# A hand-fixed order written anew, with all table sums left to TensorE, in a gated mix of a state-space convolution and linear attention

## The chip, the cores and the metric

The kernel runs on one core of one Trainium2 chip. The metric is the device time of one execution in microseconds; the median of several runs is what counts. The engines of the core are TensorE (PE in the profile, with its weight loads as PEld), VectorE (DVE), ScalarE (ACT), GpSimd (POOL) and SyncE (SP), which here only issues DMA transfers. ACT issues some DMAs too.

## What is computed

A sequence `u` of 2048 steps by 512 channels goes through two branches, and a sigmoid gate per step mixes them. Cut to what matters:

```python
# convolution branch: a kernel K of length 2048 per channel, from 128 modes
P = exp(dt * A[d, n] * l)                       # complex, n = 128, l = 0..2047
K = einsum("dn,dnl,dn->dl", C, P, dt * B).real
y = irfft(rfft(u, 2L) * rfft(K, 2L))[:L] + u * Dskip
# attention branch: 32 heads of 16, features of 32
q, k, v = x @ wqkv
phi(t) = concat(softmax(t @ w_phi), softmax(-t @ w_phi))
kv = einsum("sf,sd->fd", phi(k), v); z = phi(k).sum(s)
b = (phi(q) @ kv) / (phi(q) @ z + 1e-6) @ wo
return g * y + (1 - g) * b,  g = sigmoid((u * gate_w).sum(-1))
```

## The kernel before

The program first turns the parameters into tables, transforms `u` (PE products with small matrices of sines and cosines in place of an FFT), and makes the key side of the attention in 8 **key pairs** of two 128-step tiles. Then four **query blocks** of 512 steps run, and beside them the convolution: the 512 channels are 16 **units** of 32 channels, and four units make a **quarter** of 128 channels, which is transformed and multiplied as one (the last quarter is cut in 64, 32 and 32 channels).

One unit goes like this. PE makes arguments, ACT turns them into sines and cosines (`cs`, line 1023 and behind) and into exponentials (`E`, line 1045 for the arguments). DVE makes two products `A` of the tables C and D (line 1101, twice 1.2 us: nodes A1, A2), then adds the two halves of `A` (line 1112: node A3) or leaves that away, and makes two products `R` of `E` and `cs` (lines 1119 and 1123). PE multiplies `A` by `R` into the PSUM tile `kps` (line 183, in `kgen_chunk`): 64 small matmuls where A3 has added the halves, 128 where PE sums four terms itself. The flag `FOURS`, one digit per unit, says which. Two units share one `kps`, which is evicted into `KD`. From there on: `psA` (PE) into `XA`, `psB` (PE) into `XK`, DVE's product `t` of `XK` with the transform of `u` read back from DRAM (`XUX`, line 1233), `psz` (PE) into `Zr`, written to DRAM and read back as `ZT` (line 1287), then `psy` (PE, line 1343) and DVE's product with the gate into `xT` (lines 1365 and 1368), from which rows go out (line 1382). The last query block does its output in `bps` (line 946) and sends its rows from line 995.

In a key pair PE makes `pk`, ACT the exponentials `Ek`, and these are summed over the features of a head, into `Zk`: by two DVE reductions (line 736), or by 8 matmuls with the identity into `zk` (line 730) and one narrower reduction (line 739). The flag `ZPS`, one digit per pair, says which.

Every step is a node of the class `Plan`. No scheduler runs: `ORDER` lists all nodes in base 64, two characters each, and each engine executes its instructions in that order. `SIDES` picks the engine of each node that has a choice: evictions of PSUM on ACT or DVE (lines 149 and 151 in `copy`), output DMAs on SP or ACT, a few preparatory operations on DVE or POOL. `RINGS` picks which of two rings of PSUM buffers a tile is taken from. Buffers are counted in the line

```python
P = Plan(nc, {"XAu": 1, "UDp": 1, "xst": 2, "wT": 1, "Ek": 2, "Zk": 2, "vr": 2, "vb": 2, "acc": 1, "r8": 3, "ax": 1, "nrm": 1, "E": 2, "cs": 4, "A": 1, "R": 2,
              "KD": 1, "XA0": 1, "XK": 2, "Zr": 2, "XUX": 3, "ln": 8}, {"ps": 2, "p0": 2, "bk": 3, "acc": 1, "pf": 2})
```

so there is one buffer for `A`, two for `E`, `R`, `XK` and `Zr`, four for `cs`. The query blocks' tile `ax` shares its one buffer with `ZT`.

Of the kernel before, what the change touches and what calls it, by code (L numbers as in the profile page):

```python
# [70 lines left out]
class Plan:  # L71

    DIGITS = "0123456789abcdefghijklmnopqrstuvwxyzABCDEFGHIJKLMNOPQRSTUVWXYZ-_"
    ORDER = ("040B0H0K0d0y0C0D0L0s0I070J0M0P0g000S110j0N08010z0T0m0Q0e2R0a0p0q0r0_0W2T100U0O0V14120Y2U2x0A2S050k130Z2y2V2X2Z0R190v0t0u"
             "0b0c0w2_0l0E0X2W1516172L1a061b2Y022-30311y33340n030f0-"
             "0h1e1f0i1w2J18321c0F0o2B2K2M1n1z1H1g1A1o2D2C1d1p1I091x1E1J351Q1R2F1B0x1C2E0G2H1q36372G2I2P382N2Q391F3b2O3c4C1S3a4J4L4K4M"
             "3d3e4Q4R3f4U1Y3g4N1r4O1h4V3h1L4Y4-"
             "4P3i4Z4_3j4W4S53542z57504T3k4X1Z515b5d58521s1D593l5c3n5i5e55565j3m5a1G3o5q5f5g5s5r5t3p3r3q1T5m5n5u3s5v5h5o5k5w5x5B1P4D4E"
             "3w2v5l5p4F5y5F5C3y1U5H3x5G5I5J5z5A1V5D5E3t3z5U3D5K5V5M5N3A3R3E2w3F5W5L1O5_3G5O5Q5X5Y5Z3B3C1W605R5S1N3K3M1K3S1M5-"
             "5P3L634G642A615T653N673T6869626a666m6n6o3U6p3V3W3X3Y6b6c6q6d6r6s1t3Z3H3-1X3_3O1i1j41401_4221431-"  # L80
             "1k1l204445466e272923222b282d4748243P491m2a4a2c2e4b4g2f4c2g4d252h2o4e4h4i4n1u4j3u3v2j4p2i2l2k2m2q2p6i262s4q4o1v4k2n4u2r2t"
             "6f4v4w6j4r3I2u4x4y4z6g4l8l3J4A8p8m6t6u6k6v8q3Q4f4s6x6h8k8o6l8n8r8s6y6z6w6A6C4m4t4B8C6G8t6I6K8w8x8y8u6B6H6J4H8D8v6L6M6N7d"
             "8z8A8E4I8B7e7f8I7g8F6F9e8Q8G8H9b6O6P8R7h7j7i6Q6R8J9f7M7N8S6S6T6U6Vaeaf7O8W8X8K7k9g8L8T8U8Z8-"
             "938M8N7l6D8_7m8V7n6W6X6Y8O8P8Y7P94an7o7pao7q6_70717r90917Qa47S9295ag7R6Z7s6-"
             "72aha8a9966Ea7akaca5ai73aa75979998ajap7677a69aalatamab74ad7TaBaC7t797u7v7U78au7y7z7V7w7x9caq9naras7AavaH7W9d9h9o9paw7X9v"
             "aY9waK7Y7ZaDaL9q9raZ7a9x9y9zaIc57B7-aM9kc69D9EaQaEbX9L7Cb_aF7D9M7_9Ac07EaRaG9iaxaz80ay9B818285bYaA7Ga-"
             "7IaJ86879j9Fc19s7Jb-"
             "9l9m9Na_7bc7aNaOaPc3cbb2b37HbZc283aS9C7FaT849G9H9I9t89aUaWaV8baX7cccc8c99O9u9P9Q9R888cb87Kb9b0c4caceb19J8abacfcgbg8dck9K"
             "8ecl8f8gbbbh8hbcbibob4cP9Sbpbqcd9T8ichci7L8jcBcCcjcsdYcYctcucycDczdZd-cQcR9Ucmd_cHcvcw9W9Xcnbj9VbwbkblbxcocIbre0eLcp9Ze1"
             "e2b5b6eMbse3eUeVcxb7bye4cqbtbu9Ybdbe9-"  # L90
             "9_cAcrcSbme5cZdOdScEbfcFcGcTcUe6a0a1bve7dTdRdWeNa2e8cJcKe9bzbAedeecLeRcNcOa3eSeaebeOcMc_ePbBd0ecd1d7cVd8d9cWeCdfcXeWdPdU"
             "d2daefege-e_eQd3dbdQdgeTdVd4dndodXdhdcg1g2dieDeEdjeXbKfAbCbnbDbEbFeYfBeZf0f1bGc-dpbLddg7dqbHd5f2drbMf3f4f5bNfGbIbJbOezdk"
             "eAfDdsfEeBeIf6f7feffdldtbPdebQdBfCfHehdueifFejdmf8fgeJd6ekdvfIfJdyf9fafhfbg4fifKg5g6dwfjdzfkfcdxdCdEfLdAdFfMg3g8dGg9dHfN"
             "fleFelfdfmfpdDdLgagbgcgddIeGemeKfqeHfOfPfQfRgeenepfneofreqeresgfggghgifSfTfUfofsbRgjbSgkdJftetglfVfYfZgmgngobUbVgqfufWdM"
             "dNbWgpf-fvfxfygreufwevewexbTeydKfzfXf_g0gvgwgsgtgugx")
    SIDES = ("011111010010101011001110110010011001010100001011100000000000011000011001111101000100000100000000000000000000000010000000"
             "00100001000000000000000101010000000000000100001101001")
    RINGS = ("001010111111010010100000000000000000000000100000000000000000001101100000000101101011100100100001101010111100111001010100"
             "01111")
# [560 lines left out]
def attention_keys(P, nc, g, psum, r):  # L660
# [40 lines left out]
    for s2 in range(8):  # L701
# [20 lines left out]

        def ps4(K=K, box=box, on=P.ZPS[s2] == "1"):
            if not on:
                return
            box.ps = bank("zk")
            for u in range(2):
                e = K.E[:, u].rearrange("p g (h a b) -> p (g h) a b", a=4, b=4)
                for k in range(4):
                    nc.tensor.matmul(box.ps[:, 256 * u:256 * u + 256], lhsT=g.ident[:], rhs=e[:, :, k, :], start=(k == 0), stop=(k == 3), skip_group_check=True)  # L730

        def rd(K=K, box=box, on=P.ZPS[s2] == "1"):
            K.Z = g.kwk.tile([128, 2, 2, 32], F32, name="Zk")
            if not on:
                for u in range(2):
                    nc.vector.tensor_reduce(out=K.Z[:, u].rearrange("p g h -> p (g h)"), in_=K.E[:, u].rearrange("p g (h f) -> p (g h) f", f=16),
                                            axis=mybir.AxisListType.X, op=ALU.add)
                return
            nc.vector.tensor_reduce(out=K.Z[:].rearrange("p u g h -> p (u g h)"), in_=box.ps[:].rearrange("p (z b) -> p z b", b=4), axis=mybir.AxisListType.X, op=ALU.add)
            box.ps = None  # L740
# [294 lines left out]
def plan_exp(P, nc, g, psum, U, T, psq, deps):  # L1035

    act = g.act
    h, cc = U // 2, U % 2
    box = Bag()

    def pe():
        T.E = g.epool.tile([128, 2, 32, 32], BF16, name="E", bufs=g.P.k["E"])
        box.ps = psum([128, 2, 16, 32], "args")
        for e in range(2):
            nc.tensor.matmul(box.ps[:, e], lhsT=g.statE[64 * e:64 * e + 64, h, :], rhs=g.selE[64 * e:64 * e + 64, 16 * cc:16 * cc + 16, :],  # L1045
                             start=True, stop=True, tile_position=(64 * e, 0))
# [12 lines left out]

def plan_conv(P, nc, g, psum, r):  # L1060
# [567 lines left out]
```

## Time and profile before

| | before |
|---|---|
| median of 3 runs | 268.72 us (266.31, 268.72, 269.62) |
| span of the profiled execution, first to last instruction | 263.7 us |
| DVE busy | 233.9 us (89%) |
| ACT busy | 221.3 us (84%) |
| PE busy | 198.5 us (75%) |
| PE weight loads | 133.8 us |
| POOL busy | 8.3 us |
| moved by DMA | 35.93 MB, 136 GB/s on the mean |

The profile is that of one execution; its span is the time from its first to its last instruction, and the device time of the runs lies some us above it. Busy times are sums over one engine's instructions, so engines that run beside each other both count. In the prediction a row of the groups reads: line, engine, operation, output and input with their sizes, count, then busy us and mean ns of one, then the idle time just before them and what ended it. A row of waits reads: who waits, for whom, us in total, times, the longest. A row with two times in front is one run of instructions: when it starts (us from the start of the span) and how long it takes. SPq and ACTq are the DMA-issuing part of these engines.

### The profile page before, as it was taken

How to read it: one execution, taken by the hardware profiler on the slowest of the kernel's cores; microseconds unless marked ns; L12 is line 12 of the kernel's file. 1: busy time of each engine (PE TensorE's matmuls, PEld its weight loads, DVE VectorE, ACT ScalarE, POOL GpSimd, SP SyncE). 2: the span in 40 equal slices, each digit the busy share in tenths (PEclk: the TensorE clock that was granted, in tenths of full speed). 3: DMA queues.
4: the chain of work that ended last, by engine and by line, in shares of the span. 5: the costliest groups of instructions: out<-in, count | busy, mean ns of one | idle time of the engine just before them, and what ended most of it. 6: DMA issues, size and time to landing. Idle time of an engine off the chain costs nothing.

```text
span 263.7 us, 10050 instructions
## 1 busy us (share of the span) xinstructions
PE 198.5 (75%) x4491; PEld 133.8 (51%) x4512; DVE 233.9 (89%) x315; ACT 221.3 (84%) x305; POOL 8.3 (3%) x21
## 2 busy tenths in 40 slices
PE   0755999999845688988565867889996678979770
PEld 0654656646634423446354245665674456764550
DVE  6799989888799989999999999999999999986630
ACT  6989999998899989998999899999998996744200
POOL 4700000000000000000000000000000000000000
PEclk9999999999995659997999579999999999998975
DMA  6899000454500885203343366239753599989576
GB/s 196 144 204 233 6 4 2 121 146 138 151 10 2 239 239 165 83 13 87 88 162 82 122 209 210 73 116 199 150 193 120 189 239 242 179 206 141 133 112 102
DMA packets 67547, 35.93 MB, mean 136 GB/s; under 512 B 46000, under 2 KB 62000, under 8 KB 67504
## 3 DMA queue, kind: packets, MB, share of 16 engines
q1 hardware_dynamic: 65648, 34.76, 55.0%
q10 hardware_dynamic: 1856, 0.52, 1.1%
q8 instruction: 35, 0.57, 1.0%
q14 instruction: 8, 0.07, 0.1%
HBM read 22.17 MB, written 13.11 MB: 134 GB/s over the span
## 4 chain that ended last, share of the span: by engine, by line
PE 32%; DVE 26%; ACT 13%; DMA 12%; issue 7%; SPq 7%; DVEq 0%; ACTq 0%
PE pk L709 5%; DMA ax<-apd 5%; PE vp L757 5%; DVE A L1101 3%; SPq L1494 3%; DMA ZT<-Zd 3%; DMA apd<-apm 3%; ACT cs L68 3%; DVE R L1123 2%; DVE R L1119 2%; PE psz L1265 2%; PE psA L591 2%; PE bps L946 2%; PE psB L616 2%; PE kvp L774 2%
## 5 line engine op out<-in xcount | busy, mean ns | idle before, releaser
L1101 DVE TENSOR_TENSOR A<-Ctab,Dtab 128x2048 bf16<-128x2048 bf16 x32 | 37.9, 1220 | 0.0
L68 ACT ACTIVATE cs<-args 128x1024 bf16<-128x1024 f32 x32 | 30.8, 1042 | 1.5 <-PE args L1023 1.5
L1265 PE MATMUL psz<-t,TI 128*128 128x512 bf16 x51 | 16.5, 414 | 6.2 <-DVE t L1233 4.6
L1123 DVE TENSOR_TENSOR R<-E,cs 128x2048 bf16<-128x2048 bf16 x16 | 19.5, 1219 | 0.1
L1119 DVE TENSOR_TENSOR R<-E,cs 128x2048 bf16<-128x2048 bf16 x16 | 19.5, 1219 | 0.0
L68 ACT ACTIVATE Ek<-pk 128x512 bf16<-128x512 f32 x32 | 16.7, 600 | 1.9 <-PE pk L709 1.6
L183 PE MATMUL kps<-R,A 128*32 128x64 bf16 x1536 | 17.2, 203 | 1.5 <-DVE A L1112 0.4
L183 PEld LDWEIGHTS <-A 128*32 128x32 bf16 x1536 | 15.3, 117 | 5.6 <-issue 2.0
L149 ACT CAST Zr<-psz 128x1024 bf16<-128x1024 f32 x15 | 15.5, 1032 | 3.2 <-PE psz L1265 1.5
L149 ACT CAST XA<-psA 128x1024 bf16<-128x1024 f32 (+1 forms) x15 | 14.7, 1017 | 3.4 <-PE psA L190 3.4
L757 PE MATMUL vp<-WW,xT 128*128 128x512 bf16 x59 | 16.9, 419 | 0.5 <-issue 0.3
L616 PE MATMUL psB<-XAu,TB 64*128 64x128 bf16 x256 | 11.8, 250 | 6.6 <-ACT xst L149 3.5
L1233 DVE TENSOR_TENSOR t<-XUX,XK 128x2048 bf16<-128x2048 bf16 x14 | 16.7, 1219 | 0.0
L68 ACT ACTIVATE E<-args 128x1024 bf16<-128x1024 f32 x16 | 16.4, 1036 | 0.3 <-PE args L1045 0.2
L68 ACT ACTIVATE Eq<-pq 128x512 bf16<-128x512 f32 (+1 forms) x28 | 16.5, 694 | 0.1
L149 ACT CAST XK<-psB 128x1024 bf16<-128x1024 f32 (+1 forms) x14 | 13.7, 993 | 2.8 <-PE psB L196 1.5
L843 PE MATMUL pq<-xT,Wqp 128*128 128x512 bf16 x64 | 15.4, 379 | 0.8 <-ACT xT L149 0.6
L709 PE MATMUL pk<-WW,xT 128*128 128x512 bf16 x58 | 15.0, 380 | 0.4 <-issue 0.2
L190 PE MATMUL psA<-W,KD 128*64 128x128 bf16 x256 | 10.7, 233 | 5.5 <-ACT KD L149 2.7
L616 PEld LDWEIGHTS <-TB 64*128 64x128 bf16 x256 | 9.7, 111 | 9.9 <-issue 9.8
L196 PE MATMUL psB<-XA,TB 128*128 128x128 bf16 (+2 forms) x192 | 10.6, 206 | 3.6 <-DVE XA L151 1.6
L190 PEld LDWEIGHTS <-KD 128*64 128x64 bf16 x256 | 8.5, 117 | 9.1 <-issue 5.2
(210 smaller groups left out, 502.0 us busy)
## 6 DMA issues: line engine op xcount, KB each, us to landing
XUX<-XUd SPq DMA_DIRECT2D x32, 256.0 KB
XUd<-xst SPq DMA_DIRECT2D x8, 512.0 KB
ax<-apd SPq DMA_DIRECT2D x16, 256.0 KB
Zd<-Zr SPq DMA_DIRECT2D x15, 256.0 KB
ZT<-Zd SPq DMA_DIRECT2D x6, 512.0 KB
UD<-in_A_u_dram SPq DMA_DIRECT2D x16, 128.0 KB
XUd<-xst SPq DMA_DIRECT2D x8, 256.0 KB
wqk<-in_B_wqkv_dram SPq DMA_DIRECT2D x1, 1024.0 KB
```

Of the source, the lines that this page charges most:

```text
L68: return self.nc.scalar.activation(**kw)
L149: self.nc.scalar.copy(out=o, in_=i)
L183: nc.tensor.matmul(kps[32 * dj:32 * dj + 32, g4, e, :], lhsT=A[:, d // 4, 32 * ka:32 * ka + 32, d % 4], rhs=R[:, kr, d, :], start=(i == 0) ...
L190: nc.tensor.matmul(ps[64 * ri:64 * ri + 64], lhsT=lhsT, rhs=fc.W1[:, ri].rearrange("p r d -> p (r d)"), start=True, stop=True, tile_positi ...
L616: nc.tensor.matmul(box.ps[:, c2, sl, :], lhsT=fc.TB[rows, b0:b0 + 2].rearrange("p a b -> p (a b)"), rhs=X.t[rows, k, r0 + sl].rearrange("p ...
L709: nc.tensor.matmul(box.ps[:], lhsT=xT[:, st, kt, :], rhs=g.WW[:, kt, :], start=(kt == 0), stop=(kt == 3))
L757: nc.tensor.matmul(box.ps[:], lhsT=xT[:, st, kt, :], rhs=g.WW[:, 4 + kt, :], start=(kt == 0), stop=(kt == 3))
L1101: nc.vector.tensor_tensor(out=c.A[:, :, 64 * k:64 * k + 64, :].rearrange("p q (x b) l -> p x b q l", b=8), in0=cf.unsqueeze(2).to_broadcas ...
L1119: nc.vector.tensor_tensor(out=c.R[:, :, :, 32:64], in0=t.E[:, 1].unsqueeze(1).to_broadcast([128, 2, 32, 32]), in1=t.cs[:], op=ALU.mult)
L1123: nc.vector.tensor_tensor(out=c.R[:, :, :, 0:32], in0=t.E[:, 0].unsqueeze(1).to_broadcast([128, 2, 32, 32]), in1=t.cs[:, ::-1, :, ::-1], o ...
L1233: nc.vector.tensor_tensor(out=box.t, in0=Ls[r0 // ns].X[:], in1=box.XK[:].unsqueeze(1).to_broadcast([128, 2, 1024]), op=ALU.mult)
L1265: nc.tensor.matmul(box.ps[:, hb, :], lhsT=fc.TI[:, k].rearrange("p t h a -> p (t h a)"), rhs=box.t[:, k, 512 * hb:512 * hb + 512], start=( ...
```

## The change

`FOURS` becomes all ones, `ZPS` loses a one, and `ORDER`, `SIDES` and `RINGS` are new throughout. No other line changes; the tables take four lines less, so the lines behind them have numbers smaller by 4 in the changed kernel. The diff's core:

```diff
-    ORDER = ("040B0H0K0d0y0C0D0L0s0I070J0M0P0g000S110j0N08010z0T0m0Q0e2R0a0p0q0r0_0W2T100U0O0V14120Y2U2x0A2S050k130Z2y2V2X2Z0R190v0t0u"
...
+    ORDER = ("0H0I0s0t0u0J2L0K00190M0S0U0L0_0N110P1210130T0W0Q2x0O0B0C0D0V140g0h0i0Y0X2M0102032R2T150Z0y0z0A2J0405060R16171a2U2y0d0e0f"
...
     WARM = ("000000000000000000000000000000000000000000000000000000000000000000000000000000000000000000000000000000000000000000000000"
             "000000000000000000000")
-    FOURS = ("0111100101011000")
-    ZPS = ("01000111")
+    FOURS = ("1111111111111111")
+    ZPS = ("00000111")
```

Counted over the whole program, DVE has eight sums A3 fewer (line 1112), two reductions of line 736 more and one of line 739 fewer; PE has 512 `kps` matmuls more and 8 `zk` matmuls fewer; SP has the four DMAs of line 995 fewer and ACT has them; POOL has one operation more (`selE`, from DVE).

Three places show how the order moves. The first is VectorE near its end, the rows before the last product of the third quarter's output and the last unit; `R`, `A`, `E` and `t` are the products named above, `xT<-psy` is an output step. Before:

```order
L1365 TENSOR_TENSOR xT<-psy,gT 128x4x128
L1053 TENSOR_TENSOR E<-E,Gtab 128x1024
L1123 TENSOR_TENSOR R<-E,cs 128x64x32
L1112 TENSOR_TENSOR A<-A 128x8x256
L1233 TENSOR_TENSOR t<-XUX,XK 128x2048 x2
L1101 TENSOR_TENSOR A<-Ctab_75,Dtab 128x64x8x4 x2
L1112 TENSOR_TENSOR A<-A 128x8x256
L1053 TENSOR_TENSOR E<-E,Gtab 128x1024
L1123 TENSOR_TENSOR R<-E,cs 128x64x32
L1365 TENSOR_TENSOR xT<-psy,gT 128x4x128
L151 CAST XK<-psB 128x1024
L1368 TENSOR_TENSOR xT<-psy,gT 128x8x128
```

and with the change:

```order
L1049 TENSOR_TENSOR E<-E,Gtab 128x1024
L1097 TENSOR_TENSOR A<-Ctab_75,Dtab 128x64x8x4
L1361 TENSOR_TENSOR xT<-psy,gT 128x4x128
L1049 TENSOR_TENSOR E<-E,Gtab 128x1024
L1115 TENSOR_TENSOR R<-E,cs 128x64x32
L1119 TENSOR_TENSOR R<-E,cs 128x64x32
L1115 TENSOR_TENSOR R<-E,cs 128x64x32
L1229 TENSOR_TENSOR t<-XUX,XK 128x2048 x2
L1119 TENSOR_TENSOR R<-E,cs 128x64x32
L1097 TENSOR_TENSOR A<-Ctab_75,Dtab 128x64x8x4 x2
L1364 TENSOR_TENSOR xT<-psy,gT 128x8x128
L1361 TENSOR_TENSOR xT<-psy,gT 128x4x128
```

The two sums (line 1112) are gone, the `R` products of two units now stand together, and the pair of `A` products stands last of the table work instead of ahead of `E` and `R`.

The second is ScalarE round the last two exponentials (`E<-args`); `Zr`, `KD`, `XA` and `XK` are evictions on the path from `kps` to the output. Before:

```order
L68 ACTIVATE cs<-args 128x1024 x2
L149 CAST XK<-psB 128x1024
L65 ACT_TABLE_LOAD
L68 ACTIVATE E<-args 128x1024
L149 CAST Zr<-psz 128x2x8x64
L68 ACTIVATE E<-args 128x1024
L149 CAST KD<-kps 128x1024
L149 CAST Zr<-psz 128x2x8x64
L149 CAST XA<-psA 128x32x32 x2
L149 CAST XK<-psB 128x1024 x2
```

and with the change:

```order
L145 CAST oT_4861<-ops 128x1024
L145 CAST XK<-psB 128x1024
L68 ACTIVATE cs<-args 128x1024 x2
L65 ACT_TABLE_LOAD
L145 CAST Zr<-psz 128x2x8x64 x2
L68 ACTIVATE E<-args 128x1024
L145 CAST KD<-kps 128x1024
L68 ACTIVATE E<-args 128x1024
L145 CAST XA<-psA 128x32x32 x2
L145 CAST Ctab_74<-psy 128x4x128
L145 CAST XK<-psB 128x1024 x2
```

Both `Zr` evictions now stand ahead of the two exponentials, and `KD` between them.

The third is SyncE at its end; `Zd<-Zr` writes the third quarter's transform to DRAM, `ZT<-Zd` reads it back, `out_dram` are output rows. Before:

```order
L1278 DMA Zd_64_123<-Zr 128x1024
L1382 DMA out_dram<-xT 32x12x256 x2
L995 DMA out_dram<-xT 32x4x384 x2
L1287 DMA ZT<-Zd_64_123 64x32x32 x2
L1382 DMA out_dram<-xT 512x1x64 x4
L995 DMA out_dram<-xT 32x4x384 x2
L1382 DMA out_dram<-xT 512x1x64 x2
```

and with the change:

```order
L1378 DMA out_dram<-xT 32x12x128 x2
L1274 DMA Zd_64_123<-Zr 128x1024
L1378 DMA out_dram<-xT 32x12x128 x2
L1378 DMA out_dram<-xT 32x12x256 x2
L1283 DMA ZT<-Zd_64_123 64x32x32 x2
L1378 DMA out_dram<-xT 512x1x64 x6
```

The four transfers of line 995 are no longer on SyncE; they stand on ScalarE.

More of the change, by code (lines that the diff above doesn't have):

```diff
@@ L73 @@
     DIGITS = "0123456789abcdefghijklmnopqrstuvwxyzABCDEFGHIJKLMNOPQRSTUVWXYZ-_"
-    ORDER = ("040B0H0K0d0y0C0D0L0s0I070J0M0P0g000S110j0N08010z0T0m0Q0e2R0a0p0q0r0_0W2T100U0O0V14120Y2U2x0A2S050k130Z2y2V2X2Z0R190v0t0u"
[L75 to L99, printed above, removed]
+    ORDER = ("0H0I0s0t0u0J2L0K00190M0S0U0L0_0N110P1210130T0W0Q2x0O0B0C0D0V140g0h0i0Y0X2M0102032R2T150Z0y0z0A2J0405060R16171a2U2y0d0e0f"
+             "0j0k0l0a0b0c2S1y2V2X0708090m0n0o2K0-2Z0p0q0r1w2-1b1c1n2W0v0w0x1x1e1f2_1o1d1z1p1A2Y303118351g331q1r1s321H2B341B1E2C2H1I1C"
+             "1J362I2D371S1F2F2G1L2E2P1M2N382Q393b2O3a1D0E0F0G4C4J4L1Y1P3d3c4K3e3f4Y4M4N4O3g4Z4-3h4_1t1u1v1G4P4Q4U4R4S533j4V4W571T4T54"
+             "504X3i3k5b585c3l5d515259555e5i5j1Z5m5f5n3n3o5g565a5q5r3m5s5h4D5o5t5x3p5k5u5B1K5y4E1Q3r5l4F3q5v5p5F3R3s3t3u3v5w5C5D5H5z3w"
+             "3y5G5I3z1U5M5A5E5J5U3x3A3B3C5W5V5N5K5L2v2w3D3F3G5Q3S5O5X5_1h1i1j3K3T5R5S5Y3E635P603H3I3J5Z5-5T641R3M671N61621k1l1m696566"
+             "6m3L3U1V3N3V681W6o6a3W6n6p1O3X6b3Z3Y3O3P3Q3-6c6q4G3_6d6r6s4041424344451X1-201_272147464849222329284b6e242a4a2b2d4c2z254g"
+             "4i2f2c2e2o2A4d4e4f4j262g4h2h4k4l4m2i2q4n4o2j2p2k2l4p4q4r4s4t6t2s2m2r2t2n2u6f6u6v4u4w6x4x8n6g6i6j4v8r8l6h8p6y8k8o4y4z4A4B"
+             "6k6l6w6z6A8m8q6B6F4H4I7d8s8w6G8t8x8y8u6H8z8v6I6J9h9i9j8A8C8D8E6K8Q6L8I6M6N8B7f8F8J8R6O7e7g8G8S8Z9e9f9g6P8H7M7h7i8K7j6Q8W"
+             "8-6R6S8L6T7N6U6V6W8T8_8X8M8N7O7kae8O8Paf938U7l7m7Q7P9b9c9d8V6X6Y6Z8Y947n90anao7oa47p7R6_7071917qa8a99295ag7r7s7tap96a56-"
+             "ah72aaa7ac73ai6C6D6E75aka6at7u7v7waj7778749798ab79999aadalaB7SauamaC7x7Taq7y7z7A9n9o767UaD7Var9v9wasavaw9paK7WaL9q9xaH7a"
+             "9r9yaE9k9l9m9D7X7YaIaF7C9zaQaG7Z9s9t9u7E7F9E9L9Mc5c6axayazaAaMbXaJ7Ba_b0b1aRaN7Gb_7bc0aOaP7D7cbZc29Fcb9NaS7-7_8081828385"
+             "8687aT7I7J9G9HaUc8aVaWaXb-c38489c78bb87HbYb988bgaYaZa-9I9J9Kc18c7Kbhc98d8e9Obac4cc8f9Pcecacd9A9B9Ccfb2b3b4bick8aboch8g8h"
+             "bp7Lcgb5b6b7csci8iclcj8jctcybwdYd-cucm9Q9R9ScScTcU9T9U9VbxbqcvdZ9W9X9Ybbbjd_bce0cBbdbebfcne1czcCcwe29ZbkeUcHcoe3eVe4brcp"
+             "cDcPcQcRe5cxcIcqbyblbmbne6e7e8cAbscEcreLbtbubveMdOdS9-a0a1cFcGdTcYcZc-cJcK9_bzbAa2eWe9eaebeRcLcNcOcMc_eNa3d0d7dQd8dPeOd1"
+             "edeeefdfdUd2d9bBbCbDd3ecehcVcWcXegdgdneIeJeKdVd4d5d6dadbePeQbEbFbGeSeTdhe-eXeie_dRdodpdWdXdcdddedidjbHbIbJbKeYeZbLdqdrf0"
+             "g1bMg2fDdkdldmfAbNbOf1fBg3dsdtdufEeCeDeEf2bPf4f5f3bQfCejfGfFfHf6f7feezeAeBdvdwdxdBfffIg7f8fgfJf9fhfafig8g4g5g6dydzdAdCfK"
+             "fbfcfddEfLekdFfMfjfkfleFeGeHdDdGfNfObRbSbTg9dHgaelfmfnfofPgbgcfQfpfqfremgdgeepenfRdLdMdNfSfTfUdIdJdKgfeqerbUbVbWfsggghgi"
+             "gjgkgleogmgngoesfVfWfXfYfZf-ftfufvfwgqeteuevgpfxfyfzewexeygrf_g0gsgtgugvgwgx")
@@ L100 @@
+    SIDES = ("111101011110110010001000101000100001011100001101110000000000101010010001010100000011000100000001000000001000000000000000"
+             "01000001000000000000001000101100000000000100011000010")
+    RINGS = ("110000111110010000100000000000000000000000100000000000000010101111000000001100100101010110111011001100101011001111001011"
+             "11100")
     WARM = ("000000000000000000000000000000000000000000000000000000000000000000000000000000000000000000000000000000000000000000000000"
```

## The prediction

> **What bounds the kernel now.** The page comes first, for the engines' shares:
>
> ```profile
> span 263.7 us, 10050 instructions
> PE 198.5 (75%) x4491; PEld 133.8 (51%) x4512; DVE 233.9 (89%) x315; ACT 221.3 (84%) x305; POOL 8.3 (3%) x21
> ```
>
> VectorE (DVE) has the most work, ScalarE (ACT) only 12.6 us less. An average over stages says little, so the second view is the table of windows, cut where the first and the last table exponential (E, line 1045's `args`, evicted by ACT) start, and where the last `kps` ends:
>
> ```profile
> core 0: us, PE busy (x) PEld busy (x) DVE busy (x) ACT busy (x) POOL busy (x), PEclk, DMA share, GB/s
> 28.00:72.00 44.00, 42.91 (x752) 26.56 (x760) 38.60 (x53) 39.72 (x77) 0.00 (x0) 1.00 0.30 84
> ...
> 0.00:104.50 104.50, 78.46 (x1218) 51.44 (x1230) 93.47 (x162) 95.42 (x141) 8.33 (x21) 0.92 0.52 126
> 104.50:217.30 112.80, 87.38 (x2278) 58.00 (x2287) 110.88 (x120) 108.01 (x141) 0.00 (x0) 0.94 0.50 136
> 217.30:238.00 20.70, 18.05 (x547) 14.61 (x543) 19.37 (x19) 13.16 (x16) 0.00 (x0) 0.96 0.99 202
> 238.00:263.70 25.70, 14.66 (x472) 9.78 (x468) 10.21 (x16) 4.75 (x9) 0.00 (x0) 0.77 0.77 125
> ```
>
> The reader is to see four regimes. From 28 to 72 us (keys) PE is the full engine: 42.91 of 44. From 104.5 to 217.3 (table and convolution units) DVE is 98% busy, but ACT is 96% busy beside it: both are full at once. From 217.3 to 238.0 ACT has slack, DVE (19.37) and PE (18.05 of 20.7) have little. Behind 238 nobody is full: that is a chain of latencies. So a change that takes work from DVE alone is worth in the third row only what ACT allows, and in the fourth what PE allows. Third view, who waits for whom, ACT's rows between 104 and 217.3 us:
>
> ```profile
> ACT Zr L149 <- PE psz L1265: 1.5, 4, 0.6
> ACT XK L149 <- PE psB L196: 0.8, 1, 0.8
> ACT apm L68 <- DVE zs L886: 0.8, 2, 0.4
> ACT zs L68 <- PE zs L867: 0.7, 1, 0.7
> ACT XA L149 <- PE psA L190: 0.4, 2, 0.3
> ACT E L68 <- PE args L1045: 0.2, 1, 0.2
> ...
> PE psz L1265 <- DVE t L1233: 4.6, 5, 1.8
> PE psB L196 <- DVE XA L151: 1.6, 1, 1.6
> ```
>
> ACT idles 4.4 us there, and the last two rows (PE's, 104 to 238) say why PE was late for it: `psz` had waited for DVE's `t`, `psB` for DVE's XA eviction. So Zr 1.5, XK 0.8 and apm 0.8, 3.1 us together, come from a late DVE.
>
> **The change, part by part.** Rows by form:
>
> ```profile
> L1112 DVE TENSOR_TENSOR A<-A 128x2048 bf16<-128x2048 bf16 x8 | 9.8, 1221 | 0.1
> ...
> L1101 DVE TENSOR_TENSOR A<-Ctab,Dtab 128x2048 bf16<-128x2048 bf16 x32 | 37.9, 1220 | 0.0
> ...
> L736 DVE TENSOR_REDUCE Zk<-Ek 128x64 f32<-128x1024 bf16 x8 | 9.3, 1210 | 0.0
> ...
> L739 DVE TENSOR_REDUCE Zk<-zk 128x128 f32<-128x512 f32 x4 | 2.8, 692 | 1.4 <-PE zk L730 1.3
> ...
> L458 DVE TENSOR_TENSOR selE<-m,b 128x1024 bf16<-128x1024 bf16 x1 | 1.2, 1217 | 0.0
> ...
> L151 DVE CAST XAu<-psA 128x1024 bf16<-128x1024 f32 x8 | 9.5, 1218 | 1.5 <-PE psA L591 1.4
> ...
> L151 DVE CAST vb<-vp 128x512 bf16<-128x512 f32 x9 | 6.1, 687 | 1.9 <-PE vp L757 1.9
> ...
> L183 PE MATMUL kps<-R,A 128*32 128x64 bf16 x1536 | 17.2, 203 | 1.5 <-DVE A L1112 0.4 <-ACT XA L149 0.3 <-DVE A L1101 0.3
> ...
> L730 PE MATMUL zk<-Ek,ident 128*128 128x256 bf16 x32 | 4.2, 277 | 0.0
> ...
> L149 ACT CAST KD<-kps 128x1024 bf16<-128x1024 f32 x7 | 7.2, 1033 | 0.0
> ...
> L149 ACT CAST vb<-vp 128x512 bf16<-128x512 f32 x7 | 4.2, 596 | 1.2 <-PE vp L757 0.8 <-DVE vr L766 0.4
> ```
>
> DVE loses the eight sums on line 1112 (9.8 us) and selE (1.2, to POOL, which is busy 3%). The key pair that no longer goes over PE gives it two reductions of 1.21 for one of 0.69: +1.7. Of the evictions it gives up two wide ones (1.22 each) and seven narrow (0.69), and takes two wide, two narrow and three other copies, which I put at 0.75 each, near the narrow row: 6.1 for 7.3, -1.2. Sum **-10.5 us** of DVE work, -9.8 of it inside the units.
>
> ACT gets nothing from that. Counted by name in front of the last E, it has four wide evictions more (KD, XK, WW, a 1024-wide oT) and four fewer (two UDp, xT, XA), and three narrow more against one fewer: 2 x 0.6 = **+1.2 us** up to the last E; up to the first E the same count gives one wide more, three fewer, two narrow more: -0.8. The cover for ACT's unchanged load is nothing; it simply stays.
>
> PE gains 512 `kps` matmuls and loses 8 `zk`. By the row 17.2 / 1536 = 11.2 ns each, +5.7 and -1.05. The loss lies in the full key stage and agrees with ACT's -0.8 at the first E; I count it once. The gain lies beside ACT and DVE in a stage where PE is busy 87.38 of 112.8 us. What it costs if that cover is gone is a rival below.
>
> The Trainium skill, page "TensorE: Matmul & The Clock Gate", section "Wait — 56ns, not 53.3ns?", speaks against this change: matmuls never start closer than about 25 ns however small. An estimate by that page is 512 x 25 = 12.8 us instead of 5.7, 1.9 us more for each full unit, and with two units behind the last E a total of about 266 us. The trace disagrees: 128 `kps` in 1.26 us (row below) are 9.8 ns each, since four column strips run side by side; I keep the row.
>
> Now the path. The rows that carry it:
>
> ```profile
> 217.32 1.04 ACT L68 ACTIVATE E<-args 128x1024 bf16<-128x1024 f32 x1
> ...
> 115.88 1.26 PE L183 MATMUL kps<-R,A 128*32 128x64 bf16 x128
> ...
> 228.58 0.73 PE L183 MATMUL kps<-R,A 128*32 128x64 bf16 x64
> ...
> 241.73 1.04 PE L1265 MATMUL psz<-t,TI 128*128 128x512 bf16 x4
> ...
> 231.80 0.63 PE L1343 MATMUL psy<-ZT,TJ 64*32 64x128 bf16 x32
> ...
> 226.74 1.91 PE L932 MATMUL ops<-Eq,KVbd 128*128 128x256 bf16 x16
> ...
> 235.62 0.51 PE L1343 MATMUL psy<-ZT,TJ 64*32 64x128 bf16 x22 [1.43 <-issue]
> ...
> 220.68 1.01 ACT L149 CAST Zr<-psz 128x1024 bf16<-128x1024 f32 x1 [1.41 <-issue]
> ...
> 225.11 2.25 SPq L1287 DMA_DIRECT2D ZT<-Zd  x2
> ...
> 256.59 0.69 DVE xT L1368
> ...
> 255.97 2.63 SPq L1382 DMA_DIRECT2D out_dram<-xT  x3
> ...
> 258.64 1.10 SPq L995 DMA_DIRECT2D out_dram<-xT  x2
> ...
> 259.84 1.26 SPq L1382 DMA_DIRECT2D out_dram<-xT  x2
> ```
>
> *Up to the last E* (217.3): ACT's work +1.2, its waits for a late DVE -3.1. DVE has no say, being 9.8 us lighter. **-1.9**; bounds +1.2 (no wait goes) and -3.2 (all 4.4 go).
>
> *From there to the end of the last `kps`* (238.0): PE's own rows. Between the last `argE` and the first L946 PE now has four `psz` fewer (1.04), 32 `psy` fewer (0.63), 8 `ops` fewer (half of 1.91), and 256 `kps` in two units where it had 192 in three (2 x 1.26 - 3 x 0.73 = +0.3): -2.3. DVE's rest shrinks more: behind the last E's product it had all of units 14 and 15 mixed in, now 9.8 us with no sum. And the 1.43 us that PE idled before `psy` at 235.62 go: those waited for the third quarter's ZT read, issued at 225.11 because the last Zr of that quarter (220.68) came 3.4 us after the last E; now that Zr stands ahead of the last two E. **-3.7**; bounds 0, if PE idles elsewhere instead, and -5.2 if DVE's lead shows fully (it would be done 8.8 us earlier than the 235.5 of now, and the first step has 1.9 of that, 1.7 more go to PE's order).
>
> *The end.* PE's sequence from the last `kps` is the same, piece for piece. Swapped sides of XA, XK and Z halves stay chained one after the other: 0, within ±0.7 for one narrow eviction. But the last output rows are written at 257.3 and SP issues them only at 259.84, behind three slow issues and two of line 995 (1.10 us); those two now stand on ACT: **-1.1**. Bounds: 0 and -1.2.
>
> The page "DMA: Bandwidth & Descriptors" of the Trainium skill, section "Issuing engines are not separate DMA queues", says that a second issuing engine saves only the sequencer's time. That is the 1.10 us of the row and no more; were the issue held up by the transfers themselves (0.77 DMA share in the last window), the sum would be 1.1 us longer. The trace cannot tell the two apart.
>
> DMAs at the start: SP issues the same set of loads, the u blocks now ahead of weights and parameters. What is late for one is early for the other; I price it at 0, with bounds of ±2 us, about what two issues take in the row of line 1287 (2.25). A third XUX load now stands between the first `apm` write and its `ax` read, which so far landed just in time; 0 to +1.
>
> Sum: -1.9 - 3.7 - 1.1 = **-6.7 us**: 257.0 of span. The timed median lies 5.0 us above the profiled span (268.72 against 263.7); I carry that over: **262.0 us**.
>
> **The rivals.**
>
> *ACT keeps its waits.* Its 4.4 us idle turn into waits for PE, which has 5.7 us more to do and takes each unit's `kps` 0.53 us later. Then the last E is at +1.2, PE gives -2.3, SP -1.1: -2.2, **266.5**. For it: ACT at 96% has no room; in the row of ACT's waits four of six releasers are PE. Against it: PE was late because DVE was.
>
> *DVE's whole gain shows.* -8.8 up to its last table product, -1.1 at the end: -9.9, **258.8**. Against it ACT's 108.01 of 112.8.
>
> *One A buffer, slower.* Pool A has one buffer: the next unit's first product (L1101) waits until `kps` has read the last. That row's idle is 0.0 now, because in half of the units the sum of 1.22 us and a `kps` of 0.73 stood in between. Now `kps` lasts 1.26 (1.5 at a low clock) and starts later, behind what PE has queued: 16 `psA` (0.6), `ops` (1.0), `argE`. DVE has 1.1 to 4.3 us of other work there, some 2 on the mean. If PE comes 1.7 us late on the mean, each unit stops DVE 1.7 + 1.3 - 2 = 1.0 us, times 16 = 16, less 10.5 saved: +5.5, less SP's 1.1: +4.4, **273**. It decides from about 1.3 us on. For it: `kps` idled only 1.5 us in all 16 units, so PE mostly does come after its operands. Against it: DVE never once waited for it.
>
> *The change does less than it says* is excluded: line 1112 is gone from the program.
>
> **How the numbers follow.** Forecast 262.0: 0.37. DVE's whole gain: 0.14. ACT keeps its waits: 0.28. One A buffer: 0.21. The measurement of this kernel tells about 2% from no change, 5.4 us, so 263.3 and 274.1 are the marks. Faster by over 2% holds 258.8 and most of the forecast (0.33 of 0.37, its tail towards 264.5 left out): 0.47. Slower by over 2% takes the upper half of the A buffer's case and what I can't see in a program whose every queue is reordered: 0.19. Within 2%: 0.34. The range goes from 257.5 (DVE's whole gain, less the 1.3 of the best start) to 272.0, where the slower case is half in; the forecast's own range is 259.5 to 265.0.
>
> **What would show it.** Right: DVE about 223.5 us busy, no row on line 1112's add, ACT unchanged near 221; the last E near 215.5, the last `kps` done near 232.5, and ACT's waits for `psz` below 1 us. ACT's share must rise above DVE's loss: 98% in the middle stage. Wrong: a row "DVE A <- PE kps" of several us (the A buffer), PE waiting for ACT and ACT for PE in the middle stage with the last E behind 217, or a start of the keys that is later than 28 us, which I priced at nothing.

## The result, and the profile after

The changed kernel is slower: 283.27 us on the median of 4 runs (279.48 to 285.77) against 267.86 us (4 runs, 266.31 to 269.62) of the kernel before. The ratio is 1.049, 95% interval 1.039 to 1.059. Some executions of any kernel come out longer and are left out of all ratios here (two of these four, so that the ratio is smaller than the quotient of the medians), while the traces of two experiments, the cut matmuls and the units 5, 6, 13 and 14, are of such executions. The forecast was 262.0 us, the range 257.5 to 272.0.

The head of the profile of the changed kernel, and its windows, cut again at the first E, the last E and the end of the last `kps` (columns: the window, its length, then busy us and number of instructions of PE, PE's loads, DVE, ACT and POOL, the granted clock, DMA share and GB/s):

```profile
span 277.7 us, 11063 instructions
PE 205.8 (74%) x4994; PEld 140.5 (51%) x5016; DVE 224.9 (81%) x306; ACT 220.8 (80%) x306; POOL 10.5 (4%) x22
```

```profile
0.00:105.80 105.80, 78.97 (x1224) 52.34 (x1236) 92.16 (x165) 94.10 (x140) 10.50 (x22) 0.89 0.49 123
105.80:234.70 128.90, 97.88 (x2781) 66.29 (x2794) 110.57 (x117) 110.55 (x144) 0.00 (x0) 0.91 0.46 129
234.70:254.20 19.50, 15.84 (x538) 13.01 (x526) 14.49 (x14) 10.48 (x13) 0.00 (x0) 0.91 0.92 190
254.20:277.70 23.50, 13.09 (x469) 8.82 (x468) 7.67 (x13) 5.72 (x11) 0.00 (x0) 0.81 0.72 115
```

The busy times came out much as worked out: DVE lost 9.0 us (233.9 to 224.9), ACT kept its load, PE gained 7.3. What grew is above all one window: from the first to the last E it took 112.8 us and now takes 128.9. In it nobody is full any more: DVE is busy 110.57 us of 128.9, ACT 110.55, PE 97.88. The time went into waiting, and the waits of the whole run name the place (who waits, for whom, us in total, times, the longest):

```profile
ACT KD L145 <- PE kps L179: 9.9, 5, 2.7
...
PE kps L179 <- issue: 8.4, 4, 3.0
...
ACT Zr L145 <- PE psz L1261: 6.2, 4, 3.9
DVE A L1097 <- PE kps L179: 6.1, 6, 1.8
```

DVE and ACT wait for `kps`, 6.1 and 9.9 us, and PE itself stands in front of `kps` for 8.4 us waiting for "issue", that is for nothing that the profile shows. More rows of this kind, of `psy`, `bps` and `zs`, bring the sum to 17.1 us; before, the largest such row was 1.4 us. PE's timeline round the longest of them, and the last one (start, length, count, and in brackets the idle time in front):

```profile
164.11 1.20 PE L179 MATMUL kps<-R,A 128*32 128x64 bf16 x120
168.33 0.26 PE L179 MATMUL kps<-R,A 128*32 128x64 bf16 x8 [3.02 <-issue]
...
267.25 0.62 PE L1352 MATMUL psy<-Z,TJ 64*32 64x16 bf16 x62
270.23 0.20 PE L1352 MATMUL psy<-Z,TJ 64*32 64x16 bf16 x2 [2.35 <-issue]
```

PE stops in the middle of a unit's 128 matmuls, after 120 of them, for 3.02 us, and the profile finds nothing that it waits for. At the end it stops after 62 of 64. A late operand is hardly the reason there; the instructions themselves are late, as the following shows. They come by DMA, and the profile lists the queue that brings them (packets, MB, share of the 16 engines), here before and after:

```profile
q8 instruction: 35, 0.57, 1.0%
```

```profile
q8 instruction: 39, 0.64, 1.0%
```

Each transfer is 16,384 bytes, and 39 of them for the 10,010 recorded instructions of PE (4,994 matmuls, 5,016 loads) make one transfer for 257. Set beside each other in the trace of the changed kernel, the ten stops of PE longer than 0.5 us that follow such a transfer are these (position among PE's records, 28 of semaphores and drains counted too; end of the transfer; PE goes on; idle before):

```
  3510   124.71   125.98   1.57
  4278   144.16   145.56   0.54
  4534   148.04   149.56   1.84
  5301   166.94   168.33   3.02
  5811   183.29   184.68   1.76
  7089   206.28   207.64   1.94
  7598   225.88   227.24   2.02
  8620   246.36   247.72   1.99
  9643   264.94   266.47   0.93
  9899   268.73   270.23   2.35
```

The positions lie multiples of 256 apart, less 0 to 3 (768, 256, 767, 510, 1,278, 509, 1,022, 1,023, 256), and PE goes on 1.27 to 1.53 us behind the end of the transfer each time. The trace lacks some records, 22 matmuls against the loads by count; in the traces of the cut matmuls and of the two A buffers (below), which have 5,016 of both, all 16 of each lie exact multiples of 256 apart. In these two, from the eleventh transfer on, each transfer starts 0.6 to 4.5 us after PE has entered a page, and brings the next one. So PE's program comes in pages of 256 instructions, the transfer of a page starts only when PE has entered the page before it, and where PE is through a page before the next is there, it stands.

One of the ten is no loss: at 266.47 PE also waits for ACT's `Z`, whose second half ends at 266.42, so it would have stood without the page end. The others, with one of 0.10 us, sum to 17.1 us in the changed kernel and to 1.7 us in the kernel before. The expectations below were worked out with the tenth counted (18 us), from PE's rows without the stops, letting at least 4.0 us pass from each page end to the next.

### The profile page after: what moved, and what is told of

Read it like the earlier page. It is cut to its first block, busy times and chain, and to the rows that moved or that the text cites. A ratio compares the mean times of both kernels' runs of the same rounds, so it can differ in the third digit from the quotient of the medians.

```text
span 277.7 us, 11063 instructions
## 1 busy us (share of the span) xinstructions
PE 205.8 (74%) x4994; PEld 140.5 (51%) x5016; DVE 224.9 (81%) x306; ACT 220.8 (80%) x306; POOL 10.5 (4%) x22
## 4 chain that ended last, share of the span: by engine, by line
PE 45%; ACT 22%; DVE 13%; issue 10%; DMA 5%; SPq 1%; DVEq 0%; ACTq 0%
PE kps L179 5%; ACT cs L68 4%; PE pq L839 4%; PE pk L705 4%; PE vp L753 4%; PE psz L1261 3%; DMA wqk<-in_B_wqkv_dram 3%; ACT E L68 3%; PE psA L186 2%; DMA XUX<-XUd 2%; ACT XK L145 2%; PE psB L192 2%; ACT Zr L145 2%; PE psy L820 2%; ACT XA L145 2%
## 5 line engine op out<-in xcount | busy, mean ns | idle before, releaser
L1097 DVE TENSOR_TENSOR A<-Ctab,Dtab 128x2048 bf16<-128x2048 bf16 x32 | 38.7, 1221 | 6.1 <-PE kps L179 6.1
L179 PE MATMUL kps<-R,A 128*32 128x64 bf16 x2048 | 22.6, 204 | 11.2 <-issue 8.4
L179 PEld LDWEIGHTS <-A 128*32 128x32 bf16 x2048 | 20.3, 117 | 16.5 <-issue 11.5
L145 ACT CAST Zr<-psz 128x1024 bf16<-128x1024 f32 x14 | 14.3, 1019 | 6.4 <-PE psz L1261 6.2
L68 ACT ACTIVATE Ek<-pk 128x512 bf16<-128x512 f32 x32 | 17.1, 608 | 1.8 <-PE pk L705 1.5
L1261 PE MATMUL psz<-t,TI 128*128 128x512 bf16 x50 | 16.1, 411 | 2.8 <-ACT KD L145 0.8
L145 ACT CAST KD<-kps 128x1024 bf16<-128x1024 f32 (+2 forms) x10 | 8.3, 844 | 9.9 <-PE kps L179 9.9
L145 ACT CAST XA<-psA 128x1024 bf16<-128x1024 f32 x13 | 13.2, 1036 | 3.5 <-PE psA L186 3.5
L145 ACT CAST XK<-psB 128x1024 bf16<-128x1024 f32 (+1 forms) x16 | 15.2, 980 | 0.8 <-PE psB L192 0.8
L705 PE MATMUL pk<-WW,xT 128*128 128x512 bf16 x57 | 15.3, 380 | 0.4
L186 PE MATMUL psA<-W,KD 128*64 128x128 bf16 x256 | 11.8, 247 | 2.8 <-ACT KD L145 1.1
```

The lines of the kernel that those rows point to most:

```text
L68: return self.nc.scalar.activation(**kw)
L145: self.nc.scalar.copy(out=o, in_=i)
L179: nc.tensor.matmul(kps[32 * dj:32 * dj + 32, g4, e, :], lhsT=A[:, d // 4, 32 * ka:32 * ka + 32, d % 4], rhs=R[:, kr, d, :], start=(i == 0) ...
L186: nc.tensor.matmul(ps[64 * ri:64 * ri + 64], lhsT=lhsT, rhs=fc.W1[:, ri].rearrange("p r d -> p (r d)"), start=True, stop=True, tile_positi ...
L705: nc.tensor.matmul(box.ps[:], lhsT=xT[:, st, kt, :], rhs=g.WW[:, kt, :], start=(kt == 0), stop=(kt == 3))
L1097: nc.vector.tensor_tensor(out=c.A[:, :, 64 * k:64 * k + 64, :].rearrange("p q (x b) l -> p x b q l", b=8), in0=cf.unsqueeze(2).to_broadcas ...
```

## The experiments

Three theories stood against each other: PE's instructions come too late (theory 1); the new order itself is slow, whatever the flags (theory 2); the one A buffer makes DVE wait for a `kps` that now starts later (theory 3, the slow rival of the prediction). "Stops" are the times that PE stood at a page end, without the wait for `Z`, summed as above from the one trace of each kernel.

### The flags of before in the new order

```diff
-    FOURS = ("1111111111111111")
+    FOURS = ("0111100101011000")
```

> The changed kernel with FOURS of before: its order, sides and rings kept, 8 units with the sum on DVE (line 1112's node, +9.8 us of DVE) and 64 kps matmuls again (1,024 PE instructions fewer, weight loads included). Theory 1, PE runs out of instructions at page ends (each 16 KB fetch holds 256 of them): worked out on the changed kernel's PE rows with 4.0 us as the least time from one page end to the next, the stalls fall from 18 to about 6 us, and the time from 283 to 270 to 276. Theory 2, the new order itself is slow: 280 or more, with the stalls no measure of it. Theory 3, one A buffer: DVE's wait for kps (6.1 us) halves, about 280.

Measured: 267.69 us, ratio to before 1.006 (1.002 to 1.010). The flag alone takes nearly all of the loss away; what is left of the new order is 0.6%. PE's waits for issue in it:

```profile
PE psy L1352 <- issue: 3.1, 1, 3.1
PE kps L179 <- issue: 1.6, 1, 1.6
PE psy L822 <- issue: 0.7, 1, 0.7
```

The stops are 5.8 us (worked out: about 6), 3.4 of them in the tail. Theory 2 falls. The time is even below what theory 1 gave, 270 to 276; why is not shown.

### The new flags in the old order

```diff
-    FOURS = ("0111100101011000")
+    FOURS = ("1111111111111111")
```

> The kernel before with FOURS all ones and nothing else changed: no sum on DVE, 1,024 PE instructions more. Theory 1 (instruction pages): by the rows of before with the kps instructions added, stalls of about 11 us instead of 1.7, at the page ends inside or behind kps; time 272 to 279. Theory 2 (the new order is slow, the flag is not): 262 to 267. Theory 3 (A buffer): a wait of DVE for kps of 4 us or more that does not hang on page ends; 266 to 272.

Measured: 276.09 us, ratio 1.032 (1.025 to 1.040), with stops of 11.2 us, both as theory 1 gave them (272 to 279, about 11); the largest groups of them:

```profile
PE kps L183 <- issue: 4.4, 5, 2.1
PE psy L1343 <- issue: 3.9, 2, 2.0
PE args L1023 <- issue: 1.7, 1, 1.7
```

The flag makes the old order slow too, by 3.2%, with 9.8 us of DVE's work taken away.

### Nothing but page ends moved

```diff
+            if first == 512 and h == 0:
+                for i in range(64):
+                    dj = i % 4
+                    nc.tensor.matmul(box.ps[32 * dj:32 * dj + 32, 2, :].bitcast(F32)[:, 0:64], lhsT=g.ident[:, 0:32], rhs=g.ident[:, 0:64], start=True, stop=True,
+                                     tile_position=(0, 32 * dj), skip_group_check=True)
```

(With their loads, 64 matmuls are half a page; the second run has 128, a whole page.)

> The kernel before with 64 tiny matmuls (128 PE instructions with their loads) put in front of the first wtp transposes, where PE sits idle 7.4 us for the wqk transfer; their result goes to an unused half of the PSUM tile. Nothing else changes, only every later page end falls 128 instructions earlier in the program. Theory 1: by the rows of before with page ends moved by 128, the stalls are 7.5 us instead of 0.8 by the same working (1.7 measured), time 271 to 276. Theories 2 and 3: no change, 267 to 269.

> The same with 128 tiny matmuls (256 PE instructions, one whole page): page ends fall where they fell before. Theory 1: stalls as before, 1 to 3 us, time 267 to 270. If the pad itself cost time, or any shift of the program disturbed it, this run is slow too: 271 or more.

Measured: 268.56 us for half a page, ratio 1.007 (1.002 to 1.012), and 267.01 us for a whole page, ratio 0.999 (0.995 to 1.004). The stops were 7.7 us in the first case, for 7.5 worked out, and 4.4 in the second, where 1 to 3 were expected. A whole page costs nothing, but it should have left the page ends where they were, so 1.7 and 4.4 us also say how far one trace can lie from another, and the 7.7 alone does not prove that the place of the page ends counts. Nor do the times: 268.56 us lie within the 267 to 269 of the other theories, and the 7.7 us of stops cost only 1.8 us here, not 3 to 8. That PE has room in the units' stage with the old order and flags, and that half of the units have a sum of 1.22 us on DVE under which a late `kps` can hide, would fit, but was not tried.

### The same load, other units

```diff
-    FOURS = ("0111100101011000")
+    FOURS = ("0111111101011110")
```

and for the twin `"1111111101011100"`.

> The kernel before with the sum left to PE in four units more (5, 6, 13, 14; 12 of 16 in all): DVE -4.9 us, PE +512 instructions, nothing else changed. The units come in neighbouring pairs, so that two of them add one whole page and every page end behind the pair falls where it fell before. Theory 1 (instruction pages): stalls of about 1.1 us by the rows of before with these instructions added, as few as before; DVE's lighter load shows in part, 263 to 267 where before is 267. Theory 3 (the A buffer, each unit without a sum costs a wait): half of the 10 us of the all-ones flag, 270 to 273.

> Its twin with unit 0 in place of unit 14: the same number of sums, matmuls and PE instructions, but the page ends behind unit 0 fall half a page off. Theory 1: stalls of about 10 us by the same working; slower than its twin by 2 to 6 us, 268 to 272. Theory 3 and any theory that counts units, matmuls or DVE work: the same time as its twin within 1 us.

Measured: 269.57 us, ratio 1.004 (0.999 to 1.010), with stops of 5.9 us; and 273.70 us, ratio 1.024 (1.015 to 1.033), with stops of 12.5 us. Two kernels with the same number of sums, matmuls and instructions lie 2% apart, against the theories that count units or DVE's work (the same within 1 us), and what differs in them is which unit keeps its sum and where the page ends fall. PE's waits for issue in front of `kps` and `psA`, the first kernel and the twin:

```profile
PE psA L190 <- issue: 2.5, 1, 2.5
PE kps L183 <- issue: 2.1, 4, 0.8
```

```profile
PE kps L183 <- issue: 5.2, 3, 2.6
PE psA L190 <- issue: 3.1, 1, 3.1
```

The difference came as expected (some 5 us by the ratios, 2 to 6 forecast), the level did not: the good set was to have 1.1 us of stops and take 263 to 267 us, and did not. The working took every page at 4.0 us, and a page can take longer (last section); whether that is the reason was not tried.

### Instructions against time on PE

In the first of these kernels the eight units that had a sum get 64 matmuls and no sum; in the second these 64 stream 128 columns each. Both have the flags of before.

```diff
...
-            an.append(P.add("DVE", "A3", (lambda: None) if four else a3, an[-1:]))
+            an.append(P.add("DVE", "A3", lambda: None, an[-1:]))
```

```diff
...
+                    else:
+                        nc.tensor.matmul(kps[32 * dj:32 * dj + 32, g4, :, :], lhsT=A[:, d // 4, 32 * ka:32 * ka + 32, d % 4],
+                                         rhs=R[:, kr, d - d % 2:d - d % 2 + 2, :], start=(i == 0), stop=(i == len(terms) - 1), tile_position=(0, 32 * dj), skip_group_check=True)
```

> The changed kernel with 64 kps matmuls in the same 8 units as before but without the sum there: it leaves out half of the terms of these 8 units. DVE as light as in the changed kernel, PE with 1,024 instructions and 5.7 us fewer. Theory 1: stalls of 6 to 7 us as in the run with the flags of before, no wait of DVE for kps to speak of, 262 to 267. If DVE's lighter load is what breaks the order (it comes earlier and waits elsewhere): 270 or more.

> The same, but each of the 64 matmuls of these 8 units streams 128 columns in place of 64 (it computes something else there): PE's time about that of the changed kernel, the instructions those of the run before it. Theory 1: what costs is the number of instructions, so it stays within 3 us of that run, 263 to 269. Rival, PE's time in kps is what delays A, KD and the rest: 276 or more, near the changed kernel's 283.

Measured: 262.97 us, ratio 0.983 (0.970 to 0.995), and 262.95 us, ratio 0.985 (0.978 to 0.993), with stops of 5.3 and 4.8 us. The groups of `kps` in the second, the kept units and the wide ones:

```profile
L180 PE MATMUL kps<-R,A 128*32 128x64 bf16 x1024 | 11.3, 204 | 3.1 <-DVE A L1101 1.6 <-DVE R L1123 0.7 <-issue 0.7
L183 PE MATMUL kps<-R,A 128*32 128x128 bf16 x512 | 8.7, 220 | 0.7 <-ACT XA L145 0.5 <-DVE Zr L147 0.2
```

The 512 wide matmuls took 8.7 us, half way between the 5.7 of 512 narrow ones and the 11.3 of 1,024, and that made no difference. The changed kernel differs from this one by 2.6 us of PE's time and by 1,024 instructions, and by the ratios (1.049 against 0.985) it takes 17 us more.

### The instructions alone

```diff
...
+                    for c in ((0,) if four else (0, 32)):
+                        w = 64 if four else 32
+                        nc.tensor.matmul(kps[32 * dj:32 * dj + 32, g4, e, c:c + w], lhsT=A[:, d // 4, 32 * ka:32 * ka + 32, d % 4],
+                                         rhs=R[:, kr, d, c:c + w], start=(i == 0), stop=(i == len(terms) - 1), tile_position=(0, 32 * dj), skip_group_check=True)
```

> The new order with FOURS of before (so the sums of 8 units on DVE again), but each of the 64 kps matmuls of these units cut into two of 32 columns: the same work and the same result, the PE instructions of the changed kernel. Theory 1 (instructions alone): stalls of 10 us or more and 273 to 281, where the uncut kernel took 267.7. Rival, it is PE's time or the missing sum: 267 to 270.

Measured: 282.21 us, ratio 1.050 (1.039 to 1.061), with stops of 19.0 us; theory 1 gave 273 to 281. (Against the expectation this kernel computes something else in these units; why is open.) The groups and waits:

```profile
L181 PE MATMUL kps<-R,A 128*32 128x64 bf16 x1024 | 12.0, 204 | 10.0 <-issue 8.3 <-DVE A L1099 1.3 <-ACT cs L68 0.4
L181 PE MATMUL kps<-R,A 128*32 128x32 bf16 x1024 | 10.8, 185 | 4.5 <-DVE A L1110 2.3 <-issue 1.6 <-ACT XA L145 0.5
```

```profile
ACT KD L145 <- PE kps L181: 12.4, 5, 4.2
...
DVE A L1099 <- PE kps L181: 6.5, 3, 2.9
```

Here all sums of before stand on DVE, and the columns streamed are those of the kernel that took 267.69 us. Nearly the same work in 1,024 instructions more gives the whole loss of the change, with the same waits of DVE and ACT behind it. The half matmuls do take 10.8 us for 1,024, as narrow as they are, so this run adds 5 us on PE too; the run with wide matmuls shows that 3 us of such time cost nothing, and the other 2 us are not covered.

### Two A buffers

```diff
...
-                nc.vector.tensor_tensor(out=c.A[:, :, 64 * k:64 * k + 64, :].rearrange("p q (x b) l -> p x b q l", b=8),
+                nc.vector.tensor_tensor(out=c.A[:, :, 0:64, :].rearrange("p q (x b) l -> p x b q l", b=8),
...
-                c.A = g.wk.tile([128, 8, 128, 4], BF16, name="A", tag="A", bufs=g.P.k["A"])
+                c.A = g.wk.tile([128, 8, 64, 4], BF16, name="A", tag="A", bufs=g.P.k["A"])
...
-        P = Plan(nc, {"XAu": 1, "UDp": 1, "xst": 2, "wT": 1, "Ek": 2, "Zk": 2, "vr": 2, "vb": 2, "acc": 1, "r8": 3, "ax": 1, "nrm": 1, "E": 2, "cs": 4, "A": 1, "R": 2,
+        P = Plan(nc, {"XAu": 1, "UDp": 1, "xst": 2, "wT": 1, "Ek": 2, "Zk": 2, "vr": 2, "vb": 2, "acc": 1, "r8": 3, "ax": 1, "nrm": 1, "E": 2, "cs": 4, "A": 2, "R": 2,
```

> The changed kernel with two A buffers: both products of a unit are written to the same 64 columns so that two buffers fit, and the 128 matmuls read these twice (so what it computes in kps is something else); all durations and counts stay. Theory 1: PE still runs out of instructions, 14 to 18 us of stalls, but DVE's 6.1 us of waits for kps go; 276 to 281. Theory 3, the one A buffer is what the time hangs on: 264 to 271.

Measured: 279.37 us, ratio 1.046 (1.038 to 1.054), with stops of 20.2 us:

```profile
L1097 DVE TENSOR_TENSOR A<-Ctab,Dtab 128x2048 bf16<-128x2048 bf16 x32 | 39.0, 1219 | 0.1
L179 PE MATMUL kps<-R,A 128*32 128x64 bf16 x2048 | 23.1, 204 | 14.6 <-issue 11.7 <-DVE A L1097 1.5 <-DVE R L1119 0.7
```

DVE's 6.1 us of waits for `kps` are gone (0.1 left), and the time cannot be told from that of the changed kernel (1.049). So DVE's waits were not what the time hangs on; without them PE stands more, 11.7 us in front of `kps`. Theory 3 falls. The granted clock is no rival either: it is 0.914 in this trace, whose span is 278.3 us, and 0.916 in that of the kernel before, with 263.7 us.

### Two ways to keep the gain

```diff
-    FOURS = ("1111111111111111")
+    FOURS = ("0111111101101000")
```

> The new order with ten units summed on PE, the set (1 to 7, 9, 10, 12) for which the rows of the run with the flags of before, with 4.0 us from page end to page end, give the fewest stalls: 4.8 us against 6.0. Theory 1: 264 to 267, a little under the 267.7 of that run with two sums (2.4 us of DVE) fewer. A theory that counts units: 2/8 of the way to 283, 271 to 272.

Measured: 264.48 us (263.42 to 265.40), ratio 0.993 (0.988 to 0.997), with stops of 4.6 us for the 4.8 worked out; the largest groups:

```profile
PE psy L1352 <- issue: 3.1, 1, 3.1
PE kps L179 <- issue: 0.6, 1, 0.6
PE psy L822 <- issue: 0.5, 1, 0.5
```

The time is within the 264 to 267 that theory 1 gave, and a theory that counts units gave 271 to 272. It is the new order with the flag digits chosen by where page ends fall, and it is below both kernels, though by less than 1% of the kernel before. Its largest stop, 3.1 us, stands at the very end.

```diff
...
-                nc.vector.tensor_tensor(out=c.A[:, :, 0:64], in0=c.A[:, :, 0:64], in1=c.A[:, :, 64:128], op=ALU.add)
+                nc.gpsimd.tensor_tensor(out=c.A[:, :, 0:64], in0=c.A[:, :, 0:64], in1=c.A[:, :, 64:128], op=ALU.add)
```

> The new order with FOURS of before, the 8 sums done by GpSimd in place of DVE: same result, DVE as light as in the changed kernel, PE's instructions as few as before. No run shows what such a sum takes there. At 1 to 2 us: 262 to 266, below both kernels. At 4 us or more it stands in the chain of the one A buffer, DVE waits for it, and the time is 272 or more.

Measured: 294.37 us, one run. A sum takes 4.36 us on POOL where it takes 1.22 on DVE, PE waits for it, and DVE for the `kps` that comes late by it:

```profile
L1108 POOL TENSOR_TENSOR A<-A 128x2048 bf16<-128x2048 bf16 x8 | 34.9, 4362 | 212.7 <-ACT E L68 88.0 <-DVE A L1097 54.5 <-PE psB L192 38.4
...
PE kps L179 <- POOL A L1108: 13.9, 4, 4.9
...
DVE A L1097 <- PE kps L179: 6.2, 4, 4.3
```

## Why the prediction was wrong

*DVE's, ACT's and PE's work.* Right in the main: DVE -9.0 us for -10.5, ACT -0.5 for a load that was to stay, PE +7.3 for +4.7 (at a granted clock of 0.892, where it was 0.916).

*Up to the last E, -1.9.* This is the step that failed. The last E started at 234.68 us, 17.4 later than before. Of these, 1.3 us lie ahead of the first E (105.8 for 104.5), where the prediction counted nothing with bounds of 2 us; the traces of the new order have the first E at 105.2 to 106.7 us and those of the old at 102.6 to 106.4, so this part is not settled. The other 16.1 lie between the first and the last E. The step rested on "The gain lies beside ACT and DVE in a stage where PE is busy 87.38 of 112.8 us": PE's extra work was priced as busy time, 512 matmuls of 11.2 ns, with 25 us of room. But a unit of 128 matmuls is, with its 128 loads, a whole page of 256 instructions in 1.26 us, where some 4 us are wanted for a page. The kernels with wide and with cut matmuls show it from both sides: 3 us on PE without the instructions cost nothing (262.95 us), the instructions with the sums still on DVE cost as much as the whole change (282.21 us). The profile of before held two hints: the row `q8 instruction: 35, 0.57, 1.0%` says that PE's instructions come by DMA, and the row `235.62 0.51 PE L1343 MATMUL psy<-ZT,TJ 64*32 64x128 bf16 x22 [1.43 <-issue]`, quoted in the prediction, was such a stop: a transfer of instructions ended at 234.32, 1.30 us before PE went on. It was read there as a wait for the ZT read, and its removal was entered as a gain.

The other half of this step, 3.1 us of ACT's waits that go with a lighter DVE, failed on its own. In the two kernels with DVE as light and without the instructions (64 matmuls, narrow and wide) the last E stands at 220.4 and 219.3 us, 3.1 and 2.0 later than before, and between the first and the last E ACT waits 5.3 and 3.8 us, where it waited 4.4 before, now for PE alone.

*From the last E to the end of the last `kps`, -3.7.* It came to -1.2: 19.5 us from 234.7 to 254.2, against 20.7. In place of the stop of 1.43 us, in front of the same line's `psy`, stands one of 1.99 at 247.72.

*The end, -1.1.* It came to -2.2: 23.5 us against 25.7, although there is a stop of 2.35 us in it. The two issues moved to ACT did not show by themselves in any run.

*The sum* looks right for a kernel without the instructions, 262.0 forecast against 262.97 and 262.95 measured, but that is in part luck. These two kernels gained 3.6 and 2.2 us of span (260.1 and 261.5 for 263.7), not 6.7: they lost at the first step and gained more than forecast at the second (14.9 and 15.3 us for 20.7). What made up for it is the term of 5.0 us between span and median. It joins two things: in each execution on record the time lies some 1.8 us above its own span (279.48 and 277.7 for the changed kernel), and the remaining 3 us are by how much the profiled execution of before was faster than the median. The order cost little either way (0.6% with the old flags).

*The rivals.* "One A buffer, slower" had the sign and the row that it asked for (DVE waits 6.1 us for `kps`), at 273 us; with two buffers the row vanishes and the time stays. It was a symptom, and that this rival had the right sign is luck. "ACT keeps its waits" had PE as the releaser (in five of the six rows quoted there, not four) and not its cause.

*The rule on the rate of matmuls* of the Trainium skill, weighed in the prediction, gave 266 us for more time on PE; the changed kernel's 2,048 `kps` took 22.6 us, 11.0 ns each (11.2 before), so the row was rightly kept. The rule that bore on the case is another: the Trainium skill, page "Runtime: NRT & Kernel Launch", section "Instruction fetch mechanics", says that the sequencer fetches its program by its own DMA in blocks of 16 KiB, 256 instructions, one ahead, and that the cost of a block's end is mostly hidden. The traces agree on the size and on the fetching ahead; hidden the cost is only where a block lasts long enough, and in the changed kernel 17.1 us of it showed.

## What stays open

What share of the stops reaches the end is not settled by a rule: in the new order 11.3 us of stops more (17.1 for 5.8) went with some 11 us of time more (ratio 1.049 for 1.006), in the old order 9.5 us more (11.2 for 1.7, all ones) with 8.5, and 6.0 us more (7.7 for 1.7, old flags) with 1.8. Each sum of stops is that of one execution, and with equal page ends 1.7 and 4.4 us were seen. That PE's longer `kps` adds to it (5.6 us for the 512 matmuls, of which 3 were tried without an effect) is not excluded for the rest. The good set of units in the old order had five times the stops that were worked out. What decides when a fetch starts was not tried by itself. The last stop of the best kernel (3.1 us in front of the last two matmuls of a `psy`) remains.

## What to carry to other kernels

Count PE's instructions as well as its time: a burst of short matmuls, each with its load, can run out of program while the profile calls the engine three quarters busy. The sign is an idle time "issue" inside a run of equal instructions, at places a multiple of 256 instructions apart; then fewer and wider matmuls are worth more than the time they take (512 wide ones for 1,024 narrow ones here); work between the bursts may be too, which was not tried. A flag that trades work of one engine for instructions of another must be chosen unit by unit, since each choice moves all page ends behind it.

## What the hardware showed

Not expected: the next page of PE's program is asked for only when the page before it is entered. Over 104 page ends in the four traces with as many matmuls as loads (cut matmuls, two A buffers, ten units, sum on POOL), the transfer began 0.92 us (median) behind the entry where the DMA engines were less than 10% busy in between, and 1.75 us behind (0.3 to 4.8) where they were over 30% busy; it took 0.9 to 2.3 us, and where PE stood, it went on 1.2 to 1.9 us after it. In the 39 stops there, a page took 2.9 to 7.5 us from its entry to that of the next, 4.3 on the median; in one place (the cut matmuls, 162.69 to 167.19 us) 4.5 us passed in front of the transfer alone. A sum of 128 by 2048 bf16 values took 4.36 us on POOL and 1.22 us on DVE.
